# Retention on one core: steps of 64 tokens in bursts of 256, each burst in three parts, in place of chunks of 128 and 64

## The chip, the core and the metric

The kernel runs on one core of a Trainium2 chip. TensorE (PE in the profile) multiplies matrices into PSUM, VectorE (DVE), ScalarE (ACT) and GpSimd (POOL) do the rest, SyncE (SP) issues the DMAs. The metric is the device time of one execution in microseconds.

## What is computed

A retention (linear attention with a decay per head), then two feed-forward parts. Batch 8, 8 heads, 576 tokens, head dimension 64, so 4608 tokens of 512 columns:

```python
scores = scale * np.matmul(q, k.transpose(0, 1, 3, 2))
gamma = 1.0 - 2.0 ** (-5.0 - np.arange(H, dtype=np.float32))
rel = pos[:, None] - pos[None, :]
Dmat = np.where(rel >= 0, gamma[:, None, None] ** rel[None, :, :], 0.0)
attn = np.matmul(scores * Dmat[None, :, :, :], v)          # then tokens x 512
h = np.maximum(np.maximum(x @ w1, x @ w2), x @ w3);  x = h @ w_out
a = x @ w1;  b = x @ w2;  out = ((a * b) @ w3) @ w_out      # second set of weights
```

## The kernel before

The retention is computed chunk by chunk with a running state. `chunk_list` cuts the 4608 tokens into chunks of 128, and of 64 where a batch (576 tokens) or a block of 512 tokens ends. For a chunk, TensorE computes the scores of its own keys and queries (L414), VectorE multiplies them with a triangular mask (`decay`, L421), TensorE multiplies them with v (`own_output`, L429) and adds what earlier chunks contribute through the state (`state_output`, L436); `gather` (L449) multiplies k with v to what the chunk adds to the state, and `update` (L455, L457) adds that to the state and multiplies it with the decay over the chunk. Decays are folded into q (`scale_q`, L394) and v (`scale_v`, L397) beforehand, on POOL. q and k come turned, by VectorE's transpose of 32x32 squares (`turn`, L400). The result lies in PSUM (tile `o`) and is split by `x_hi` (ACT) and `x_lo` (DVE) into two parts for the products that follow. All matmuls of the retention are float32, on quarters or halves of the array: scores and state output use 64 rows by 64 columns, own output and gather 128 rows (the keys) by 64 columns for chunks of 128.

The first feed-forward part (`products`, L537) runs block by block, nine blocks of 512 tokens, 18 products of twelve 128x512 matmuls each; `maximum` (L547) reads them. What runs beside it is ordered by a plan: `when(t, step)` gives a step a due time, counted in products, and the steps are emitted in order of time. Each engine works through its steps in that order. For the first two blocks (the opening, `EARLY`) the order is written out by hand in `ORDER`; a `+` there takes the next step of the plan.

Behind the opening the 31 remaining chunks (25 of 128 tokens, 6 of 64) go in pairs, the bursts. Everything that TensorE has to do for one burst stands together: at `t_o` gather, own output and state output of a pair, and with them (`t = behind`, the `t_o` of the burst before) the scores of the pair after it. So TensorE leaves the products 17 times: 16 times for a burst, with the first scores by themselves. The due times around it are 10.5 products ahead of the scores for the fetch of q and k, 5 for scaling q, 0.6 to 1.6 behind the scores for the decays, 8.5 ahead of the output for v and k, 3.5 for scaling v. Where the two chunks of a pair belong to different batches, q and k are fetched and turned for each by itself.

PSUM: products, scores and gathered sums share six banks in turn; `o` has two banks of its own, for one burst at a time. While products run, the weights of the later parts are converted from float64 on ACT and DVE (L179 to L188, L245). Later parts (L768 on) aren't touched.

Of the kernel before, what the change touches and what calls it, by code (L numbers as in the profile page):

```python
# [9 lines left out]
F32 = mybir.dt.float32  # L10
# [12 lines left out]
P = 128  # L23
# [15 lines left out]
eq8 pr0.7 mx0.6 up7 sl9 jn9 wo11 sc7 kp0.1 mx0.7 + hi9 sl10 sc8 pr0.8 + da7 wo12 db7 da8 db8 ou7 lo9 jn10 mx0.8 hi10  # L39
ga8 pr0.9 ft14 xh7 lo10 ft15 xl7 kp0.2 ft16 up8 ou8 mx0.9 + + + pr0.10 xh8 xl8 + pr1.0 mx0.10 sl11 jn11 wo13 pr1.2  # L40
sl12 ft17 mx1.0 sl13 hi11 wo14 lo11 pr1.6 sl14 wo15 jn12 wo16 jn13 pr1.3 jn14 mx1.6 hi12 hi13 lo12 hi14 pr1.1 lo13
mx1.3 lo14 sl15 jn15 wo17 pr0.11 mx1.1 hi15 mx1.2 lo15 kp1.0 sl16 pr1.5 mx0.11 jn16 kp0.3 sl17 hi16 pr1.4 lo16 jn17
hi17 pr1.9 mx1.4 mx1.5 lo17 kp1.1 pr0.12 mx1.9 pr1.7 mx0.12 + + + + mx1.7 + + + pr1.8 + + + + + pr0.15 mx1.8 + kp1.2
pr0.17 + + + + pr0.16 mx0.15 + mx0.16 + + mx0.17 kp0.5 + + + + + + + pr0.14 + + + pr1.10 + + + + + + + + pr0.13 mx1.10
pr1.12 mx0.13 mx0.14 + kp0.4 + + + + + pr1.11 mx1.12 + + mx1.11 + + + kp1.3 + + + + + + + pr1.15 + + + + + + + + + + +
pr1.16 mx1.15 + + + + pr1.13 + + + + mx1.16 pr1.14 mx1.13 + + + + pr1.17 mx1.14 + kp1.4 + + + + + + + mx1.17 + kp1.5 +
+ + + + + + + + + + + + + + + + +
# [20 lines left out]
JOINT = ((128,), (128, 128), (128, 64), (64, 128))  # L68
JOINT_AT = [sum(sum(x) for x in JOINT[:n]) // 32 for n in range(len(JOINT) + 1)]


def decay_tables():

    gamma = 1.0 - 2.0 ** (-5.0 - np.arange(H))
    i = np.arange(P)
    own = gamma.reshape(2, G)[i // D]
    qs = np.zeros((P, JOINT_AT[-1], G))
    sd = np.zeros((P, 2, G))
    for n, sizes in enumerate(JOINT):
        R = sum(sizes) // 32  # L80
        for T in range(R):
            at = i % 32 * R + T
            at = np.where(at < sizes[0], at, at - sizes[0])
            qs[:, JOINT_AT[n] + T] = own ** at[:, None] / np.sqrt(D)
    for j, c in enumerate((128, 64)):
        sd[:, j] = own ** c
    vd = gamma[None, :] ** -i[:, None].astype(np.float64)
# [7 lines left out]
def tile_retention_maxout_bilinear(ctx: ExitStack, tc, a, out):  # L95
# [170 lines left out]
    n_q = JOINT_AT[-1]  # L266
    tables = cst.tile([P, (n_q + 2) * G + H], F32, name="tables")
    qs = tables[:, :n_q * G].rearrange("p (T h) -> p T h", h=G)
    sd = tables[:, n_q * G:(n_q + 2) * G].rearrange("p (j h) -> p j h", j=2)
    vd = tables[:, (n_q + 2) * G:]  # L270
# [8 lines left out]
    def below(dst, base, rows, op=ALU.is_ge):  # L279
        nc.gpsimd.affine_select(out=dst, in_=dst, compare_op=op, fill=0.0, base=base, pattern=[[1, P]], channel_multiplier=-rows)  # L280
# [12 lines left out]
    def make_mask():  # L293
        nc.gpsimd.memset(mask, 1.0)
        below(mask, 0, 1)

# [32 lines left out]
    def attend(n, t=None, t_o=None, slot=0, pair=None, sizes=None):  # L329
        pair = {} if pair is None else pair  # L330
# [9 lines left out]

        def raw_qk(x):
            return double(x, t, 8, G, 32)[:, 4 * slot:4 * slot + R]

        def turned_qk(x):
            v = double(x + "t", t, 2, G, P, **{"bufs": 1} if x == "k" else {}).rearrange("p s h t -> p (s h t)")
            if sizes and len(sizes) == 2:
                return v[:, :G * 32 * R].rearrange("p (h t) -> p h t", h=G)
            return v[:, G * P * slot:G * P * slot + G * c].rearrange("p (h t) -> p h t", h=G)

        def fetch_qk():  # L350
            for x in "qk":
                for g in range(2):
                    for e in range(2):
                        o = D * g + 32 * e
                        load(raw_qk(x)[o:o + 32], a[x][b, G * g:G * g + G, t0:t0 + 32 * R, 32 * e:32 * e + 32].rearrange(
                            "h (t T) d -> t T h d", T=R))

        def fetch_kv():
            fetch_v()
            if not last:  # L360
                kn = at.tile([P, H, D], F32, tag="kn", name="kn", bufs=4)
                load(kn[:c], a["k"][b, :, t0:t0 + c, :].rearrange("h t d -> t h d"))
                z["kn"] = kn.rearrange("p (g h) d -> p g h d", g=2)
# [28 lines left out]
        def scale_q():  # L392
            q, at_T = raw_qk("q"), JOINT_AT[JOINT.index(sizes)]
            nc.gpsimd.tensor_tensor(q, q, qs[:, at_T:at_T + R].unsqueeze(3).to_broadcast([P, R, G, 32]), ALU.mult)  # L394

        def scale_v():
            nc.gpsimd.tensor_tensor(z["v"], z["v"], vd.unsqueeze(2).to_broadcast([P, H, D]), ALU.mult)  # L397

        def turn(x):
            nc.vector.transpose(out=turned_qk(x).rearrange("p h (t T) -> p T h t", T=R), in_=raw_qk(x))  # L400

        def take():
            at_t = sizes[0] if slot and len(sizes) == 2 else 0
            for x in "qk":
                z[x + "t"] = turned_qk(x)[:, :, at_t:at_t + c]

        def scores():
            if t is not None:
                take()
# [59 lines left out]
        if t is None:  # L469
            steps = dict(fk=(fetch_pairs, "k", "kn"), fq=(fetch_pairs, "q", "q"), fv=(fetch_v,), tk=(swap, "k"), tq=(swap, "q"),  # L470
                         ek=(settle, "k"), eq=(settle, "q"), sc=(scores,), da=(decay, 0), db=(decay, 1), sv=(scale_v,),
                         ou=(output,), xh=(x_hi,), xl=(x_lo,))
            if not last:
                steps.update(ga=(gather,), up=(update,))
            for kind, step in steps.items():
                early(f"{kind}{n}", *step)
            return
        lag = 2.0 * slot
        R = sum(sizes) // 32
        follows = slot == 1 and len(sizes) == 2  # L480
        if not follows:
            when(max(t - 10.5, 4.4) + lag, fetch_qk)
            when(t - 5 + lag, scale_q)
            when(t - 4.8 + lag, turn, "q")
            when(t - (2.8 if len(sizes) == 2 else 4.7) + lag, turn, "k")
        when(t_o - 8.5 + 0.75 * lag, fetch_kv)
        when(t, scores)
        when(t + 0.6 + 0.35 * lag, decay, 0)
        when(t + 0.9 + 0.35 * lag, decay, 1)
        if not last:  # L490
            when(t_o - 0.04, gather)
            when(t_o - 0.035 if slot == 0 else t_o + 0.5, update)
        when(t_o - 3.5 + 0.5 * lag, scale_v)
        when(t_o - 0.03, own_output)
        if not first:
            when(t_o - 0.01 if slot == 0 else t_o + 0.005, state_output)
        when(t_o + 0.5 + 0.25 * lag, x_hi)
        when(t_o + 1 + 0.25 * lag, x_lo)

    by_block = {}  # L500
    for n, (b, t0, *_) in enumerate(chunks):
        by_block.setdefault((b * S + t0) // N1, []).append(n)
    due = []
    for t, ns in by_block.items():
        for i, n in enumerate(ns):
            if t < EARLY:
                attend(n)
            else:

                due.append((n, t, T_BLK * (t - 1) - 0.52 + T_BLK * i / len(ns)))  # L510
    bursts = []
    for m in reversed(range(0, len(due), 2)):
        some = due[m:m + 2]
        t_o = min(some[-1][2], T_BLK * some[0][1] - 2.52, bursts[0][0] - 7 if bursts else NT)
        bursts.insert(0, (int(t_o + 0.52) - 0.52, some))
    behind = bursts[0][0] - 9
    for t_o, some in bursts:
        t_o = min(t_o, behind + 8) if behind > 0 and t_o != bursts[0][0] else t_o
        pair = {}
        own = tuple(chunks[n][2] for n, _, _ in some)  # L520
        joint = len(some) == 2 and chunks[some[0][0]][0] == chunks[some[1][0]][0]
        for slot, (n, _, _) in enumerate(some):
            attend(n, behind, t_o, slot, pair, own if joint else own[slot:slot + 1])
        behind = t_o
# [843 lines left out]
```

## Time and profile before

| | us |
|---|---|
| median of 3 runs | 1216.07 (1215.03 to 1216.69) |
| the profiled execution | 1216.72 |
| its span, first to last instruction | 1215.0 |
| TensorE busy | 1205.9 |
| VectorE busy | 915.8 |
| ScalarE busy | 507.1 |
| GpSimd busy | 304.3 |

The opening lasts until about 76 us, the nine blocks of products until about 530 us; the retention's last work for TensorE stands at 488 us. Busy time counts when an engine had an instruction in work. Matmuls overlap in the array, so the cost of one on TensorE is the distance from its start to the next start, not its duration.

### The profile page before, as it was taken

Reading aid. Unit: us, or ns where it says so; the run is one execution under the profiler, and the core shown is the slowest. Engines: PE = TensorE matmul, PEld = TensorE weight load, DVE = VectorE, ACT = ScalarE, POOL = GpSimd, SP = SyncE. Lnnn points to the kernel's source line nnn. Section 1 sums busy time; section 2 is a strip of 40 time slices with the busy share of each in tenths; the row PEclk is TensorE's granted clock in tenths of the full one; section 3 lists DMA queues with packets and bytes.
Section 4 is the critical chain, followed back from the end, with each engine's and each line's share of the span. In section 5 each row is a group of like instructions: output and inputs, shape, how many; then the busy total and the mean of one; then the engine's idle time right before and its main releaser. Section 6 shows DMA issues by size and latency. Waiting matters only on the chain. (4 is left out here: it accounts for less than half of the span.)

```text
span 1215.0 us, 22807 instructions
## 1 busy us (share of the span) xinstructions
PE 1205.9 (99%) x8900; PEld 1079.6 (89%) x8900; DVE 915.8 (75%) x1236; ACT 507.1 (42%) x873; POOL 304.3 (25%) x246
## 2 busy tenths in 40 slices
PE   8999999999999999999999999999999999999998
PEld 6888888888888888888889888888998888999998
DVE  5896767777768888467998467775766777998996
ACT  3661232323322322234566454443443344555554
POOL 2201212112111110000000315544244442344443
PEclk9999999999999999999999999999999999999999
DMA  9957799988987784534743733324233324455553
GB/s 206 245 143 136 189 227 206 229 191 200 209 221 166 172 206 121 175 113 165 236 172 130 252 129 131 122 105 135 101 113 130 137 66 145 156 166 168 179 166 105
DMA packets 303824, 199.36 MB, mean 164 GB/s; under 512 B 207330, under 2 KB 261346, under 8 KB 303716
## 3 DMA queue, kind: packets, MB, share of 16 engines
q1 hardware_dynamic: 303716, 197.90, 58.6%
q8 instruction: 70, 1.15, 0.4%
q14 instruction: 38, 0.31, 0.1%
HBM read 131.79 MB, written 66.06 MB: 163 GB/s over the span
## 5 line engine op out<-in xcount | busy, mean ns | idle before, releaser
L537 PE MATMUL ps_h<-xh,w1h 128*128 128x512 f32 (+1 forms) x664 | 250.4, 379 | 0.0
L537 PE MATMUL ps_h<-xh,w1l 128*128 128x512 f32 (+1 forms) x664 | 247.7, 375 | 0.5 <-DVE w1l L103 0.3
L537 PE MATMUL ps_h<-xl,w1h 128*128 128x512 f32 (+1 forms) x664 | 167.2, 375 | 0.0
L537 PEld LDWEIGHTS ps_h<-xh,w1h 128*128 128x128 f32 x664 | 125.7, 189 | 19.5 <-issue 2.2
L537 PEld LDWEIGHTS ps_h<-xh,w1l 128*128 128x128 f32 x664 | 126.0, 190 | 17.0 <-DVE w1l L103 1.0
L537 PEld LDWEIGHTS ps_h<-xl,w1h 128*128 128x128 f32 x664 | 124.0, 190 | 16.7
L547 DVE TENSOR_TENSOR hb<-ps_h,hb 128x512 f32<-128x512 f32 (+1 forms) x110 | 74.8, 680 | 74.1 <-PE ps_h L537 56.5
L1222 POOL TENSOR_TENSOR c<-c 128x512 f32<-128x512 f32 (+1 forms) x60 | 82.8, 1380 | 169.4 <-DVE c L1214 131.1
L1209 ACT ACTIVATE snap<-ps_x 128x512 f32<-128x512 f32 (+1 forms) x100 | 55.4, 554 | 158.8 <-PE ps_x L768 148.7
L100 ACT ACTIVATE hb<-ps_h 128x512 f32<-128x512 f32 (+1 forms) x56 | 32.5, 580 | 178.9 <-PE ps_h L537 178.9
L397 POOL TENSOR_TENSOR v<-v,tables 128x512 f32<-128x512 f32 x40 | 44.3, 1110 | 167.9 <-DMA v<-in_v_dram 148.7
L100 ACT ACTIVATE xh<-o 128x512 fp32r<-128x512 f32 (+1 forms) x40 | 22.2, 554 | 131.8 <-PE o L436 94.2
L179 ACT ACTIVATE e<-raw 128x512 f32<-128x512 f32 x64 | 55.4, 866 | 23.6 <-DMA raw<-in_moe_w_out_dram 8.2
L421 DVE TENSOR_TENSOR p<-sc,mask 128x512 f32<-128x512 f32 (+1 forms) x80 | 48.4, 629 | 13.7 <-PE sc L414 13.5
L394 POOL TENSOR_TENSOR q<-q,tables 128x512 f32<-128x512 f32 (+2 forms) x19 | 28.9, 1520 | 107.4 <-DMA q<-in_q_dram 97.3
L180 ACT ACTIVATE r<-raw 128x512 int32<-128x512 uint32 x64 | 54.8, 857 | 0.0
L188 DVE SCALAR_TENSOR_TENSOR m<-raw,m 128x512 int32<-128x512 int32 x64 | 53.3, 836 | 0.5
L185 DVE CUSTOM_DVE_ANT_0 m<-m,r 128x1024 uint16<-128x1024 uint16 x64 | 48.1, 752 | 7.3 <-ACT r L180 0.4
L103 POOL TENSOR_TENSOR ol<-raw,oh 128x512 fp32r<-128x512 f32 x1 | 1.3, 1277 | 205.1 <-ACT oh L100 205.1
L1214 DVE TENSOR_TENSOR c<-ps_x,snap 128x512 f32<-128x512 f32 (+1 forms) x40 | 25.2, 635 | 35.2 <-ACT snap L1209 11.1
L1214 DVE TENSOR_TENSOR c<-ps_v,snap 128x512 f32<-128x512 f32 (+1 forms) x40 | 24.8, 633 | 27.3 <-PE ps_v L768 12.9
L768 PE MATMUL ps_x<-t4h,a 128*128 128x512 f32 (+1 forms) x160 | 44.0, 360 | 0.3 <-DVE a L103 0.3
(305 smaller groups left out, 3269.9 us busy)
## 6 DMA issues: line engine op xcount, KB each, us to landing
raw<-in_moe_w_dram SPq DMA_DIRECT2D x50, 512.0 KB, 5.2
zr<-g_d SPq DMA_DIRECT2D x18, 1024.0 KB, 6.0
g_d<-c SPq DMA_DIRECT2D x64, 256.0 KB, 2.3
zr<-z_d SPq DMA_DIRECT2D x28, 512.0 KB, 6.1
h_d<-hb SPq DMA_DIRECT2D x54, 256.0 KB, 4.1
b<-h_d SPq DMA_DIRECT2D x16, 768.0 KB, 6.1
out_dram<-ob SPq DMA_DIRECT2D x35, 256.0 KB, 2.0
v<-in_v_dram SPq DMA_DIRECT2D x32, 256.0 KB, 5.5
```

The source lines that it names most:

```text
L100: nc.scalar.activation(dst, src, AF.Copy)
L179: nc.scalar.activation(z["e"], raw[:, :, 1].bitcast(F32), AF.Copy, scale=2.0 ** -112)
L180: nc.scalar.activation(z["r"], raw[:, :, 0].bitcast(U32), AF.Copy, scale=2.0 ** -29)
L185: nc.vector.tensor_tensor(z["m"], z["m"], z["r"], ALU.add)
L188: nc.vector.scalar_tensor_tensor(z["m"], z["hi"], -0x80000000, z["m"], ALU.bitwise_and, ALU.bitwise_or)
L397: nc.gpsimd.tensor_tensor(z["v"], z["v"], vd.unsqueeze(2).to_broadcast([P, H, D]), ALU.mult)
L421: nc.vector.tensor_tensor(z[g][:c, :, :c], z["sc"][g][:c, :, :c], mask[:c, :c].unsqueeze(1).to_broadcast([c, G, c]), ALU.mult)
L537: nc.tensor.matmul(ps[:, cols], l, r, start=n == 0, stop=n == len(mms) - 1)
L547: nc.vector.tensor_tensor(hb, unwoven(ps[:, cols]), hb, ALU.max)
L1209: nc.scalar.activation(t, unwoven(ps[:, :size]), AF.Copy)
L1214: nc.vector.tensor_tensor(r, unwoven(ps[:, :size]), t, ALU.add)
L1222: nc.gpsimd.tensor_tensor(x, x, y, ALU.mult)
```

## The change

Behind the opening the retention runs in steps of 64 tokens (`C`), nine to a batch (`SUBS`), and bursts are 256 tokens aligned to half blocks, whatever batch they lie in: 14 bursts of four steps. A burst holds two slots of 128 tokens with two steps each. Scores are computed only within a step (64 by 64); with `e = 1` own output takes one pairing of steps and heads, with `e = 0` the other, both on quarters of the array; the gather takes one step's 64 keys, also on quarters. The state is kept after every step, within a burst without multiplying it: decays count from the burst's start, in the tables for q (256 positions) and v (two slots), and only the burst's last update multiplies with the decay over 256 tokens. Steps that begin a batch have no state output, and those that close one no gather.

Each burst has three parts in TensorE's order, each between products: scores at `t_s` (2 behind the output of the burst before), gather and own output for `e = 1` at `t_g = t_s + 3`, state output and own output for `e = 0` at `t_o`. A copy of one column on ACT (`order`) stands between the two parts that write `o`. The upper half of the mask's first 64 columns is repeated in its lower half (`make_squares`). The places of `+` in `ORDER` change: 100 in place of 113. The opening's own steps (`attend_first`) stay as they were.

```diff
+C = 64
+SUBS = S // C
+R_T = 8
...
+def pieces_of(t0, size):
+    out, at = [], 0
+    while at < size:
+        b, t = divmod(t0 + at, S)
+        n = min(size - at, S - t)
+        out.append((b, t, n, at))
+        at += n
+    return out
...
+    at = i[:, None] % 32 * R_T + np.arange(R_T)
+    qs = own[:, None] ** at[:, :, None] / np.sqrt(D)
+    sd = np.stack([own ** c for c in (128, 64, 256)], 1)
+    vd = np.stack([gamma[None, :] ** -(e * P + i[:, None]).astype(np.float64) for e in range(2)], 1)
...
+    own_first = [(0, 0), (1, 1), (0, 1), (1, 0)]
+    squares = mask[:, :C]
...
+        def fetch_qk():
+            for x in "qk":
+                z[x] = at.tile([P, R_T, G, 32], F32, tag=x, name=x)
+                for g in range(2):
+                    for e in range(2):
+                        for b, t0, size, first in pieces_of(n * PAIR, PAIR):
+                            o = D * g + 32 * e + first // R_T
+                            load(z[x][o:o + size // R_T], a[x][b, G * g:G * g + G, t0:t0 + size, 32 * e:32 * e + 32].rearrange(
+                                "h (t T) d -> t T h d", T=R_T))
...
+        def scores():
+            z["sc"] = [bank("sc").rearrange("p (n h t) -> p n h t", n=2, h=G) for g in range(2)]
+            for slot in range(2):
+                for h in range(G):
+                    for g, s in own_first:
+                        nc.tensor.matmul(z["sc"][g][rows_of(s), slot, h], of("kt", g, h, slot, s), of("qt", g, h, slot, s), start=True, stop=True)
...
+        def gather():
+            z["st"] = [bank("st").rearrange("p (n h d) -> p n h d", n=2, h=G) for s in range(2)]
+            for slot in range(2):
+                for h in range(G):
+                    for g, s in own_first:
+                        if not closes(4 * n + 2 * slot + s):
+                            nc.tensor.matmul(z["st"][s][rows_of(g), slot, h], z["kn", slot][rows_of(s), g, h],
+                                             z["v", slot][rows_of(s), G * g + h], start=True, stop=True)
+
+        def own_output(e):
+            if e == 1:
+                z["o"] = attn_ps.tile([P, 2, 2, G, C], F32, tag="o", name="o")
+            for slot in range(2):
+                for r in range(2):
+                    for s in range(2):
+                        g = s ^ e
+                        for u in range(2):
+                            h = 2 * r + u
+                            nc.tensor.matmul(z["o"][rows_of(u), g, slot, 2 * r + s], z["v", slot][rows_of(s), G * g + h], z[g][rows_of(s), slot, h],
+                                             start=e == 1 and slot == 0 and r == 0, stop=slot == 1 and r == 1, skip_group_check=e == 0)
+            if e == 1:
+                nc.scalar.activation(order, z["o"][:, 0, 1, 3, :1], AF.Copy)
+
+        def state_output():
+            for slot, s, m in subs:
+                if begins(m):
+                    continue
+                for r in range(2):
+                    for g in range(2):
+                        for u in range(2):
+                            h = 2 * r + u
+                            nc.tensor.matmul(z["o"][rows_of(u), g, slot, 2 * r + s], before[m][rows_of(g), h], of("qt", g, h, slot, s),
+                                             start=False, stop=False, skip_group_check=True)
...
+            if not begins(m):
+                nc.vector.tensor_tensor(new, sums, before[m], ALU.add)
+                if ends:
+                    nc.vector.tensor_tensor(new, new, ratio, ALU.mult)
+            elif ends:
+                nc.vector.tensor_tensor(new, sums, ratio, ALU.mult)
+            else:
+                nc.scalar.activation(new, sums, AF.Copy)
...
+        when(max(t_s - 10.5, 4.4), fetch_qk)
+        when(t_s - 5, scale_q)
+        when(t_s - 4.8, turn, "q")
+        when(t_s - 2.8, turn, "k")
+        when(t_s, scores)
+        when(t_s + 0.6, decay, 0)
+        when(t_s + 0.9, decay, 1)
+        when(t_g, gather)
+        when(t_g + 0.01, own_output, 1)
+        for i, sub in enumerate(subs):
+            when(t_g + 0.5 + 0.3 * i, update, *sub)
+        when(t_o, state_output)
+        when(t_o + 0.01, own_output, 0)
+        for slot in range(2):
+            when(t_g - 8 + 1.5 * slot, fetch_kv, slot)
+            when(t_g - 3 + slot, scale_v, slot)
+            when(t_o + 0.5 + 0.5 * slot, x_hi, slot)
+            when(t_o + 1 + 0.5 * slot, x_lo, slot)
...
+    for n in reversed(range(EARLY * N1 // PAIR, NT // PAIR)):
+        t, i = divmod(n * PAIR, N1)
+        t_o = min(T_BLK * (t - 1) + 3.48 + T_BLK * i // N1, bursts[0] - 9 if bursts else NT)
+        bursts.insert(0, t_o)
```

## Rows read from the trace of the kernel before

**Rows 1.** The page: busy us per engine, and TensorE's granted clock in 40 slices

```profile
PE 1205.9 (99%) x8900; PEld 1079.6 (89%) x8900; DVE 915.8 (75%) x1236; ACT 507.1 (42%) x873; POOL 304.3 (25%) x246
...
PEclk9999999999999999999999999999999999999999
```

**Rows 2.** Waits of PE: who waited for whom, us in total, times, longest

```profile
PE sc L414 <- DVE qt L390: 1.4, 2, 1.0
```

**Rows 3.** Windows: length, busy us (instructions) of PE, PEld, DVE, ACT, POOL; clock, DMA, GB/s

```profile
150.00:200.00 50.00, 50.00 (x461) 44.04 (x460) 35.74 (x52) 15.90 (x23) 9.49 (x10) 1.00 0.98 225
...
400.00:440.00 40.00, 40.00 (x347) 35.18 (x345) 35.89 (x45) 11.73 (x17) 5.61 (x6) 1.00 0.78 174
```

**Rows 4.** Chain of work that ended last: start us, us, twelve matmuls of 128x512

```profile
902.41 2.59 PE ps_x L768 x12
```

**Rows 5.** Groups by line and shape on PE, 100 to 490 us: busy us, mean ns

```profile
L537 PE MATMUL ps_h<-xh,w1h 128*128 128x512 f32 x480 | 183.9, 383 | 0.0
L537 PE MATMUL ps_h<-xh,w1l 128*128 128x512 f32 x480 | 182.2, 380 | 0.0
L537 PE MATMUL ps_h<-xl,w1h 128*128 128x512 f32 x481 | 123.6, 380 | 0.0
L414 PE MATMUL sc<-qt,kt 64*64 64x128 f32 x800 | 25.1, 270 | 0.0
```

**Rows 6.** Timeline of PE around the first scores: start us, us until its end

```profile
104.94 1.03 PE L537 MATMUL ps_h<-xl,w1h 128*128 128x512 f32 x4
105.90 1.98 PE L414 MATMUL sc<-qt,kt 64*64 64x128 f32 x64
107.80 0.48 PE L537 MATMUL ps_h<-xh,w1h 128*128 128x512 f32 x1
108.12 0.38 PE L537 MATMUL ps_h<-xh,w1l 128*128 128x512 f32 x1
```

**Rows 7.** Timeline of PE, one full burst

```profile
334.31 1.15 PE L449 MATMUL st<-v,kn 128*64 128x64 f32 x32
335.30 1.92 PE L429 MATMUL o<-p,v 128*64 128x128 f32 x32
337.14 0.67 PE L436 MATMUL o<-qt,s 64*64 64x128 f32 x16
337.63 1.93 PE L414 MATMUL sc<-qt,kt 64*64 64x128 f32 x64
339.38 0.62 PE L436 MATMUL o<-qt,s 64*64 64x128 f32 x16
```

**Rows 8.** Timeline of PE, state output with 64 columns and what follows it

```profile
208.26 0.46 PE L436 MATMUL o<-qt,s 64*64 64x64 f32 x16
208.54 0.40 PE L414 MATMUL sc<-qt,kt 64*64 64x128 f32 x8
```

**Rows 9.** Timeline of PE in the opening, with a stall named in brackets

```profile
29.14 0.67 PE L436 MATMUL o<-qt,s 64*64 64x128 f32 x16 [0.73 <-issue]
```

**Rows 10.** Groups by line and shape on DVE, 100 to 490 us

```profile
L421 DVE TENSOR_TENSOR p<-sc,mask 128x512 f32<-128x512 f32 x50 | 33.4, 685 | 11.3 <-PE sc L414 11.2
...
L400 DVE STREAM_TRANSPOSE kt<-k 128x1024 f32<-128x1024 f32 x6 | 12.4, 2067 | 0.0
...
L457 DVE TENSOR_TENSOR s<-s,tables 128x256 f32<-128x256 f32 x18 | 10.0, 557 | 0.6
...
L400 DVE STREAM_TRANSPOSE kt<-k 128x512 f32<-128x512 f32 x6 | 9.5, 1586 | 0.0
...
L455 DVE TENSOR_TENSOR s<-st,s 128x256 f32<-128x256 f32 x18 | 7.6, 422 | 15.8 <-PE st L449 12.9 <-PE o L436 2.8
L421 DVE TENSOR_TENSOR p<-sc,mask 64x256 f32<-64x256 f32 x12 | 4.7, 405 | 0.0
L457 DVE TENSOR_TENSOR s<-st,tables 128x256 f32<-128x256 f32 x6 | 2.5, 421 | 5.4 <-PE st L449 5.4
```

**Rows 11.** Timeline of DVE behind the scores that end at 339.38

```profile
345.97 0.72 DVE L421 TENSOR_TENSOR p<-sc,mask 128x512 f32<-128x512 f32 x1
```

More of the change, by code (lines that the diff above doesn't have):

```diff
@@ L65, in chunk_list @@
     return out
-JOINT = ((128,), (128, 128), (128, 64), (64, 128))
-JOINT_AT = [sum(sum(x) for x in JOINT[:n]) // 32 for n in range(len(JOINT) + 1)]
+C = 64
[9 more added lines that the diff above has]
+    return out
 def decay_tables():
@@ L260, in tile_retention_maxout_bilinear @@
         add(EARLY * T_BLK - 6.5 + u * ((n_blk - 1 - EARLY) * T_BLK + 2.5) / len(rest))
[L266 to L270, printed above, removed]
+    tables = cst.tile([P, (R_T + 3) * G + 2 * H], F32, name="tables")
+    qs = tables[:, :R_T * G].rearrange("p (T h) -> p T h", h=G)
+    sd = tables[:, R_T * G:(R_T + 3) * G].rearrange("p (j h) -> p j h", j=3)
+    vd = tables[:, (R_T + 3) * G:].rearrange("p (j h) -> p j h", j=2)
+    order = cst.tile([P, 1], F32, name="order")
     mask = cst.tile([P, P], F32, name="mask")
@@ L279, in below @@
     def below(dst, base, rows, op=ALU.is_ge):
-        nc.gpsimd.affine_select(out=dst, in_=dst, compare_op=op, fill=0.0, base=base, pattern=[[1, P]], channel_multiplier=-rows)
+        nc.gpsimd.affine_select(out=dst, in_=dst, compare_op=op, fill=0.0, base=base, pattern=[[1, dst.shape[-1]]], channel_multiplier=-rows)
     def warm():
@@ L295, in make_mask, with make_squares @@
         below(mask, 0, 1)
+    def make_squares():
+        nc.gpsimd.memset(mask[C:, :C], 1.0)
+        below(mask[C:, :C], 0, 1)
     def load_rows():
@@ L327, in double, with attend_first @@
         return doubles[tag, key]
-    def attend(n, t=None, t_o=None, slot=0, pair=None, sizes=None):
-        pair = {} if pair is None else pair
+    def attend_first(n):
+        pair, slot, t = {}, 0, None
         b, t0, c, first, last = chunks[n]
@@ L339, in attend @@
         z = {}
[L341 to L363, printed above, removed]
         def fetch_v():
@@ L390, in settle @@
                 nc.vector.tensor_tensor(z["qt"][:, :, :c], z["qp"][:, :, :c], turned[:, :, :c], ALU.mult)
-        def scale_q():
-            q, at_T = raw_qk("q"), JOINT_AT[JOINT.index(sizes)]
-            nc.gpsimd.tensor_tensor(q, q, qs[:, at_T:at_T + R].unsqueeze(3).to_broadcast([P, R, G, 32]), ALU.mult)
         def scale_v():
[L397 to L405, printed above, removed]
+            nc.gpsimd.tensor_tensor(z["v"], z["v"], vd[:, 0].unsqueeze(2).to_broadcast([P, H, D]), ALU.mult)
         def scores():
-            if t is not None:
-                take()
             z["sc"] = [bank("sc").rearrange("p (h t) -> p h t", h=G) for g in range(2)]
@@ L467, in x_lo @@
             low(nc.vector, parts(xl), z["o"][:, :, :, :c], parts(xh))
[L469 to L489, printed above, removed]
@@ L490, in attend @@
-        if not last:
[L491 to L507, printed above, removed]
-            else:
-                due.append((n, t, T_BLK * (t - 1) - 0.52 + T_BLK * i / len(ns)))
-    bursts = []
[L512 to L524, printed above, removed]
+        steps = dict(fk=(fetch_pairs, "k", "kn"), fq=(fetch_pairs, "q", "q"), fv=(fetch_v,), tk=(swap, "k"), tq=(swap, "q"),
+                     ek=(settle, "k"), eq=(settle, "q"), sc=(scores,), da=(decay, 0), db=(decay, 1), sv=(scale_v,),
+                     ou=(output,), xh=(x_hi,), xl=(x_lo,))
@@ new lines, in attend_first, with rows_of, begins, closes @@
+        if not last:
+            steps.update(ga=(gather,), up=(update,))
+        for kind, step in steps.items():
+            early(f"{kind}{n}", *step)
+    n_first = 0
+    while chunks[n_first][0] * S + chunks[n_first][1] < EARLY * N1:
+        attend_first(n_first)
+        n_first += 1
+    own_first = [(0, 0), (1, 1), (0, 1), (1, 0)]
+    squares = mask[:, :C]
+    def rows_of(x):
+        return slice(D * x, D * x + D)
+    def begins(m):
+        return m % SUBS == 0
+    def closes(m):
+        return m % SUBS == SUBS - 1
@@ L527, in tile_retention_maxout_bilinear @@
+    bursts = []
+    for n in reversed(range(EARLY * N1 // PAIR, NT // PAIR)):
+        t, i = divmod(n * PAIR, N1)
+        t_o = min(T_BLK * (t - 1) + 3.48 + T_BLK * i // N1, bursts[0] - 9 if bursts else NT)
+        bursts.insert(0, t_o)
+    t_s = bursts[0] - 9 + 2
+    when(t_s - 6, make_squares)
+    when(t_s, hand_over)
+    for n, t_o in enumerate(bursts):
+        attend(EARLY * N1 // PAIR + n, t_s, t_s + 3, t_o)
+        t_s = t_o + 2
     hbs = {}
```

83 lines of the change are left out of this document (63 added, 20 removed).

## The prediction

> **What bounds the kernel now.** The page comes first. TensorE is busy for 1205.9 of the 1215.0 us, at the full granted clock in every slice, while VectorE has a quarter of the span free [rows 1]. So I ask whether TensorE is held up by anyone, and the waits of PE say hardly: the longest entry in total is 1.4 us, in the opening [rows 2], and from 76 to 490 us the view lists none. In the windows of the stretch that the change rewrites (100 to 490 us) PE is busy for all of every window, while DVE goes up to 35.89 of 40 us and the DMA engines to 0.98 [rows 3]. TensorE's own stream sets the time there: whatever is taken out of it comes off the end, as long as VectorE and the DMAs still deliver.
>
> A busy PE is not yet a price list, since one matmul's duration (380 ns) holds the filling and draining that its neighbours overlap. I price by start to start. Twelve 128x512 matmuls take 2.59 us, so 0.2157 us each [rows 4]. In 100 to 490 us there are 480 + 480 + 481 = 1441 of them [rows 5], 310.8 us; the other 390 - 310.8 = 79.2 us belong to attention. Summing the 17 visits of attention to TensorE, each from where the next product would have started, gives 79.4 us; I use that.
>
> A float32 matmul is two instructions: 25 chunks of 128 with 16 score matmuls each make x800 [rows 5]. What one costs is read from a visit:
> - Scores alone, 64 instructions of 64x64 with 128 columns: the last four products start at 104.94, so the next would at 105.80; scores start at 105.90, the next product at 107.80, and the one after it 0.32 instead of 0.216 later [rows 6]. That is 2.00 + 0.10 = 2.10 us. In the middle of a visit 64 such instructions take 337.63 to 339.38 = 1.75 us, sixteen rounds of 0.109 us in which the four quarters of the array work side by side [rows 7]. So a visit costs 2.10 - 1.75 = **0.36 us** beside its columns.
> - Own output, 128 rows by 64: only two side by side. 32 instructions take 335.30 to 337.14, 1.84 us, sixteen pairs of 0.109 us and 0.09 for the change of tile shape [rows 7].
> - The gather has 64 columns: 32 instructions in 0.99 us, with 0.05 for the visit's first pair [rows 7], so 0.058 to 0.059 us a pair; I use 0.0584, at which the check below closes.
> - State output with 64 columns, four quarters: 16 instructions from 208.26 to 208.54 [rows 8], 0.28 us of which 0.05 is the first round after a change of shape; 0.058 us a round.
>
> Check on the whole: scores 800/4 x 0.1092 + 96/2 x 0.0584 = 24.6 us; own output (400 and 96 instructions, in pairs) 24.6; state output (320 and 80, in fours) 9.9; gather (336 + 48, in pairs) 11.2. Together 70.4 us. The remaining 9.0 us are 17 visits: 0.36 for the first and 0.51 for most of the others, which change from the 128x64 to the 64x64 shape on the way (0.15). The prices close.
>
> **The change, part by part, on TensorE.** There are 14 bursts of 256 tokens, 56 steps of 64.
> - Scores: 32 matmuls of 64 columns a burst, 64 instructions, 16 rounds; 14 x 16 = 224 rounds. The score blocks above the diagonal go.
> - Own output: both parts together 64 instructions, now 64x64 and so four side by side: 224 rounds.
> - Gather: 64 instructions a burst. The 7 steps that close a batch are left out, but they idle half the array for their slot and save no round: 224.
> - State output: 50 steps (6 begin a batch) of 16 instructions, 200 rounds.
>
> 872 rounds x 0.0584 = 50.9 us against 70.4. The gain is in scores and own output (24.6 to 13.1 each); gather and state output get dearer by 1.9 and 1.8 us.
> - Visits: 14 bursts in three separated parts are 42 instead of 17. Nothing in them has the 128x64 shape, so I take 0.36 each: 15.1 us against 9.0. The bounds are 0.33 (first visit with a quicker tail) and 0.51.
>
> Sum: 50.9 + 15.1 = 66.0 us against 79.4, **13.4 us less**.
>
> What each quarter sustains is the unknown that matters: 64-column rounds of four stand in the trace only 16 instructions long; now 64 to 128 follow each other. The near bound is 0.058 us a round, the far one the rate of the long runs of scores, 1.75/64 = 27.3 ns an instruction [rows 7]. I take the near one, as it is the same shape and count of columns, and because after the one stall for instructions (0.73 us in the opening) the state output ran on at its usual rate [rows 9].
>
> One rule of the Trainium skill speaks against this. The trace shows 16 instructions of 64 columns in 0.28 us, 17.5 ns each [rows 8]. The skill (TensorE: Matmul & The Clock Gate, The HAM clock gate) says that starts never come closer than about 25 ns however small N is, and TensorEngine Tiling (Instruction Overhead) warns not to take the tiling from a dimension that is already small. By 25 ns the 3376 new instructions would take an estimated 84 us instead of 51; across the quarters the row contradicts it.
>
> **The other engines.** VectorE: 62 decays (33.4 + 4.7 us) become 28 of about 0.685, 19.2 us [rows 10]. The updates go from 20.1 us to about 25 (43 adds at 0.42 and some 13 multiplications at 0.42 to 0.557 [rows 10]). Transposes and the low parts stay within a few us. So VectorE gets lighter by some 15 to 20 us, which is hidden: PE doesn't wait for it. Four first steps move to ScalarE, a quarter busy there, with 14 one-column copies that only order writes. POOL loses its memsets and gains one small mask step ahead of the first scaling of q, far from its use. SP issues about as many transfers (214 instead of 213 for q, k and v by my count), of the same short packets; I price them at nothing, hidden by lead times as long as before (5 products from fetch to scaling). If that cover fails, PE waits at the gather.
>
> New waits on PE: the first part of own output comes three products after the scores, and waits for the decay on VectorE. Until then 3 x 2.59 + 0.36 + 0.93 = 9.1 us pass. Now the last decay of a burst ends at 346.69, 7.3 us after its scores [rows 11], and that one is planned later than the new one, which needs no second slot. The cover shrinks from some 15 us to several, but holds. Queued behind that wait on PE would be the next products. State output waits for three updates, four products (10.4 us) after the gather; before the change it waits inside the visit, where only the scores cover it. The opening loses 13 places for later work and gets others; there VectorE loses a transpose (three at about 1.58 become one of 2.06 in one place [rows 10]). I take zero, bounds minus 1 and plus 3 us.
>
> **The sum against the times.** The profiled execution is 1216.72 us, 1.72 beyond its span; less 13.4 that is 1203.3. It lies 0.65 above the median of 1216.07, so the time is 1216.07 - 13.4 = **1202.7 us**. I count 0.2% (2.4 us) as what a measurement of this kernel tells from no change.
>
> **The rivals.**
> 1. The quarters don't hold their rate (slower). After 16 instructions of a part, the rest go at 27.3 ns: 672 x 14.6 + 2704 x 27.3 ns = 83.6 us, with visits 98.7, so 19.3 us more: 1235. It decides where the mean goes over (79.4 - 15.1)/3376 = 19.0 ns. For it: no long run shown, and more instructions per us than anywhere. Against: four rounds at full rate [rows 8]. The skill's 25 ns, named above, gives an estimated 1236 in the same way. Chance 0.06.
> 2. New waits. Three parts a burst with shorter cover, VectorE at 0.9 in 400 to 440 us and the DMAs near full [rows 3]. If each of the 14 bursts loses 0.3 to 0.8 us, plus up to 3 in the opening: 4 to 14 us, so 1207 to 1217. Chance 0.11.
> 3. Visits at the dear price: 42 x 0.15 = 6.3 us more, 1209. Against: the 0.15 belongs to the 128x64 shape, which is gone. Chance 0.08.
> 4. A little more gain: visits at 0.33, an opening with less idle time: 1200 to 1201. Chance 0.03.
>
> **How the numbers follow.** The forecast has 0.72, with a range of its own of 1200.5 to 1206 (rounds up to 0.063, visits 0.33 to 0.38). Faster by over 0.2% holds it, rivals 3 and 4 and most of rival 2: 0.89. Within 0.2%: the end of rival 2, 0.04. Slower: rival 1 and a little of 2, 0.07. The range is 1199.5 to 1210, which leaves out rival 1 and the upper part of rival 2.
>
> **What the changed profile would show.** Right: PE still without waits behind the opening; 42 visits; 64 scores of 64 columns in about 0.93 us and a visit with them alone in 1.3; gather and own output 1.9 us; the rest of the kernel alike but earlier by 13 us. Wrong: rounds of 64 columns well over 0.06 us (rival 1); PE idle at the own or state output with DVE named, or at the gather with POOL or a DMA (rival 2); visits whose start and tail exceed 0.36 us (rival 3).

## The result, and the profile after

The changed kernel takes **1202.85 us** (median of 6 runs, 1200.65 to 1204.52) against 1216.38 for the kernel before beside it (6 runs, 1214.47 to 1218.76): a ratio of 0.989, 95% interval 0.987 to 0.991. The forecast was 1202.7. The profiled execution took 1202.30 us, 1.7 of it beyond its span of 1200.6.

The page of the changed kernel, to be laid beside [rows 1]:

```profile
PE 1191.8 (99%) x10100; PEld 1059.9 (88%) x10100; DVE 894.8 (75%) x1202; ACT 506.3 (42%) x888; POOL 298.1 (25%) x228
...
PEclk9999999999999999999999999999999999999999
```

TensorE is still the engine that is never free: 14.1 us less busy, with 1200 matmuls and as many weight loads more. Who is waited for, beside [rows 2]:

```profile
PE sc L386 <- DVE qt L376: 1.7, 3, 1.0
...
PE sc L521 <- DVE kt L511: 1.1, 1, 1.1
```

The second row is the only wait in attention behind the opening. The groups of attention on TensorE, 95 to 482 us (busy us, mean ns, idle before), beside [rows 5]:

```profile
L546 PE MATMUL o<-p,v 64*64 64x64 f32 x896 | 18.9, 219 | 0.0
L521 PE MATMUL sc<-qt,kt 64*64 64x64 f32 x896 | 16.3, 221 | 1.1 <-DVE kt L511 1.1
L534 PE MATMUL st<-v,kn 64*64 64x64 f32 x784 | 16.2, 222 | 0.0
L559 PE MATMUL o<-qt,s 64*64 64x64 f32 x800 | 14.9, 221 | 0.0
```

The counts are those of the prediction, all in one shape. (784 is the gather without the closing steps.) One burst, in the timeline of PE (start us, us until its end), beside [rows 7]:

```profile
123.63 0.81 PE L639 MATMUL ps_h<-xl,w1h 128*128 128x512 f32 x3
124.37 1.16 PE L521 MATMUL sc<-qt,kt 64*64 64x64 f32 x64
125.47 0.48 PE L639 MATMUL ps_h<-xh,w1h 128*128 128x512 f32 x1
125.79 0.38 PE L639 MATMUL ps_h<-xh,w1l 128*128 128x512 f32 x1
...
129.89 1.03 PE L639 MATMUL ps_h<-xl,w1h 128*128 128x512 f32 x4
130.84 1.16 PE L534 MATMUL st<-v,kn 64*64 64x64 f32 x64
131.82 0.65 PE L546 MATMUL o<-p,v 64*64 64x64 f32 x32
132.40 0.48 PE L639 MATMUL ps_h<-xh,w1h 128*128 128x512 f32 x1
...
137.78 1.16 PE L559 MATMUL o<-qt,s 64*64 64x64 f32 x64
138.76 0.65 PE L546 MATMUL o<-p,v 64*64 64x64 f32 x32
```

Read start to start, as in the prediction. The three matmuls of a product at 123.63 would let a fourth start at 124.28; scores start 0.09 later, the next matmul of a product at 125.47, and the one after it 0.32 instead of 0.216 later: 1.29 us for the visit. By the prices of the prediction it is sixteen rounds of 0.0584 (0.93) and a visit of 0.36. Gather with own output takes 1.75 us in the same way, state output with own output 1.76.

Over the whole trace, from the span's start to the start of TensorE's last matmul, 1211.69 us became 1197.33, **14.36 less**. Attention behind the opening went from 79.42 us in 17 visits to 66.95 in 42, which is 12.47. The opening gave about 1.6 us, all the rest 0.3.

### The profile page after: what moved, and what is told of

The parts are those of the page before. It is cut to its first block, busy times and chain, and to the rows that moved or that the text cites. A ratio compares the mean times of both kernels' runs of the same rounds, so it can differ in the third digit from the quotient of the medians.

```text
span 1200.6 us, 25154 instructions
## 1 busy us (share of the span) xinstructions
PE 1191.8 (99%) x10100; PEld 1059.9 (88%) x10100; DVE 894.8 (75%) x1202; ACT 506.3 (42%) x888; POOL 298.1 (25%) x228
## 3 DMA queue, kind: packets, MB, share of 16 engines
q8 instruction: 79, 1.29, 0.5%
## 4 chain that ended last, share of the span: by engine, by line
PE 95%; DVE 2%; DMA 1%; ACT 1%; issue 0%; SPq 0%; DVEq 0%; POOL 0%; ACTq 0%; POOLq 0%
PE ps_h L639 35%; PE ps_x L870 23%; PE ps_y L870 11%; PE ps_v L870 6%; PE ps_X L870 5%; PE ps_w L870 3%; PE ps_Y L870 3%; PE ps_V L870 1%; PE sc L521 1%; PE st L534 1%; PE o L546 1%; PE o L559 1%; PE o L401 1%; PE sc L386 1%; DMA raw<-in_moe_w_out_dram 1%
## 5 line engine op out<-in xcount | busy, mean ns | idle before, releaser
L507 POOL TENSOR_TENSOR v<-v,tables 128x512 f32<-128x512 f32 x28 | 31.0, 1108 | 223.5 <-DMA v<-in_v_dram 204.0
L186 ACT ACTIVATE r<-raw 128x512 int32<-128x512 uint32 x64 | 52.2, 815 | 0.0
L503 POOL TENSOR_TENSOR q<-q,tables 128x1024 f32<-128x1024 f32 x14 | 27.6, 1970 | 96.7 <-DMA q<-in_q_dram 68.9
L870 PE MATMUL ps_v<-b21h,a 128*128 128x512 f32 (+1 forms) x160 | 43.8, 359 | 0.1
```

Of the source, the lines that this page charges most:

```text
L186: nc.scalar.activation(z["r"], raw[:, :, 0].bitcast(U32), AF.Copy, scale=2.0 ** -29)
L507: nc.gpsimd.tensor_tensor(v, v, vd[:, slot].unsqueeze(2).to_broadcast([P, H, D]), ALU.mult)
L870: nc.tensor.matmul(ps, l, r, start=start and j == 0, stop=stop and j == len(mms) - 1, skip_group_check=again)
```

## The experiments

The theory was that of the prediction: the time follows TensorE's stream, 0.0584 us for a round of four quarters and 0.36 us for each visit. The rivals were that the quarters lose their rate in long runs (rival 1), and that new waits or VectorE set the time (rival 2). All line numbers are those of the changed kernel, moved by a line or three where an edit adds some. The kernel before, beside which each was timed, took 1215.29 us (19 runs) for the repeat, the doubled scores, and two visits and one visit a burst; 1215.76 (7 runs, on another chip) for the doubled decays, four visits, and the two kernels that change from the third burst on; 1217.36 (one run) for the last two. Between these groups the ratios are to be compared, not the times.

**The changed kernel once more**, for an equal to compare with.

> The changed kernel as it is, timed beside the three others on the same chip: 1202.9 by every theory. It is the base for the differences of e1, e2 and e3.

1201.21 us (1200.7 to 1202.42), ratio 0.988 (0.986 to 0.989). Attention takes 65.79 us in 42 visits and there is no wait in it behind the opening: the one of 1.1 us above belongs to a single execution. In that one the timeline of DVE reads

```profile
139.75 0.43 DVE L190 TENSOR_SCALAR m<-e 128x512 int32<-128x512 int32 x1 [2.98 <-ACT e L185]
140.51 0.69 DVE L191 CUSTOM_DVE_ANT_0 m<-m,r 128x1024 uint16<-128x1024 uint16 x1 [0.33 <-ACT r L186]
141.12 2.06 DVE L511 STREAM_TRANSPOSE kt<-k 128x1024 f32<-128x1024 f32 x1
```

that of ACT

```profile
139.04 0.68 ACT L185 ACTIVATE e<-raw 128x512 f32<-128x512 f32 x1 [6.27 <-DMA raw<-in_moe_w_out_dram]
```

and that of PE

```profile
143.33 1.16 PE L521 MATMUL sc<-qt,kt 64*64 64x64 f32 x64 [1.13 <-DVE kt L511]
```

The transposition of k stood behind a conversion step on VectorE that waited 2.98 us for ScalarE, and ScalarE waited for a transfer. This is rival 2's mechanism, once, for 1.1 us.

**Each score product twice.** If the quarters fall back in runs longer than 16, 128 instructions in a row cost far more than twice 64.

```
-                    for g, s in own_first:
+                    for g, s in own_first + own_first:
```

> The changed kernel with every score matmul behind the opening issued twice (the second writes the same values): 896 instructions of 64 columns more, in runs of 128 instructions. If TensorE's stream sets the time and the quarters hold their rate in long runs: 224 rounds x 0.0584 = 13.1 us more than the changed kernel, about 1216, which is the time before. If long runs fall to 27.3 ns an instruction: 24.5 us more or above. If TensorE has hidden slack: clearly less than 13 us.

1215.47 us (10 runs, 1213.88 to 1217.54), ratio 1.000 (0.999 to 1.001): 14.3 us above the changed kernel. Attention takes 78.81 us, 13.02 more, as expected; the opening, which the edit doesn't touch, ended 2.0 us later in this trace than in that of the repeat (first scores behind it at 108.57 and 106.61). The timeline of PE:

```profile
127.01 2.09 PE L521 MATMUL sc<-qt,kt 64*64 64x64 f32 x128
129.04 0.48 PE L639 MATMUL ps_h<-xh,w1h 128*128 128x512 f32 x1
129.36 0.38 PE L639 MATMUL ps_h<-xh,w1l 128*128 128x512 f32 x1
```

128 instructions start within 129.04 - 127.01 = 2.03 us, where 64 took 125.47 - 124.37 = 1.10: 0.93 us for 64 more, 14.5 ns each. By rival 1's 27.3 ns they would have taken 1.75. Rival 1 falls.

**VectorE charged with 19 us.** Every decay is computed twice, which takes VectorE back to more than it did before the change.

```
-            nc.vector.tensor_tensor(z[g]..., squares..., ALU.mult)
+            for _ in range(2):
+                nc.vector.tensor_tensor(z[g]..., squares..., ALU.mult)
```

> The changed kernel with each of its 28 decays behind the opening issued twice on VectorE (same values), 28 x 0.68 = 19 us more there, about what the change takes off VectorE. If TensorE's stream alone sets the time: as the changed kernel, 1201.2 in the last comparison, within 1.5 us. If the lighter VectorE carried a part of the gain: 3 us more or above, with waits of TensorE that name VectorE.

1202.77 us (1200.79 to 1202.99), ratio 0.989 (0.987 to 0.991): by the ratio no different from the changed kernel (0.988 in the repeat); by the time 1.56 above it, just over the 1.5 expected. Attention takes 65.75 us, again without a wait behind the opening; here too the opening ended 2.0 us later (108.64). VectorE is busy for 916.7 us, 0.9 more than before the change. What VectorE saves by the change is hidden, as forecast, and so is that much more.

**Four visits a burst.** The first part of own output goes one product further back, away from the gather.

```
-        when(t_g + 0.01, own_output, 1)
+        when(t_g + 1.01, own_output, 1)
```

> The changed kernel with the first part of own output a product behind the gather, so that a burst has four visits: 56 instead of 42, the same columns. Price of 0.36 us a visit: 14 x 0.36 = 5.0 us more than the changed kernel, 1206.2. If visits are free: 1201.2. Shorter runs of instructions can't stall more on the supply of instructions, so nothing else is expected to change.

1206.6 us (1205.33 to 1207.27), ratio 0.993 (0.991 to 0.994). Twelve visits more are found, not the 14 expected (in two bursts the two parts stood together all the same), and attention takes 70.01 us: (70.01 - 65.79)/12 = **0.352 us a visit**, with the same instructions. A visit costs what the prediction said, measured by itself.

**Two visits a burst.** If 0.35 us are paid for each visit, fewer should pay. Scores of the next burst directly behind the state and own output:

```
+    t_g = t_s + 3
...
-        attend(EARLY * N1 // PAIR + n, t_s, t_s + 3, t_o)
-        t_s = t_o + 2
+        attend(EARLY * N1 // PAIR + n, t_s, t_g, t_o)
+        t_s, t_g = t_o + 0.02, t_o + 5
```

> The changed kernel with the scores of the next burst placed directly behind the second part of own output, so that they share a visit; everything else of a burst is timed as in the changed kernel. TensorE leaves the products 29 times instead of 42. If the stream of TensorE sets the time and a visit costs 0.36 us beside its columns: 13 x 0.36 = 4.7 us less than the changed kernel, about 1198. If the gain of the change came from the lighter VectorE, with TensorE only seeming busy, fewer visits bring nothing: 1203. If the changed kernel has hidden waits at the visits, more than 4.7 us comes back or a new wait takes it.

1199.91 us (1198.32 to 1200.54), ratio 0.986 (0.985 to 0.988). Attention takes 63.59 us in 29 visits. That holds a stall of 1.8 us inside one visit, which the waits name "issue", and the opening ended about 2 us later than in the repeat of the changed kernel (first scores behind it at 108.83 and 106.61); kernels whose opening has the same order vary as much. So of 4.6 us for 13 visits saved, attention shows 2.2 and the median 1.3.

**One visit a burst**, all parts one behind the other, the updates moved with them. In one line of `ORDER` some places of `+` move too.

```
-        when(t_g + 0.01, own_output, 1)
+        when(t_o, own_output, 1)
...
-            when(t_g + 0.5 + 0.3 * i, update, *sub)
-        when(t_o, state_output)
-        when(t_o + 0.01, own_output, 0)
+            when(t_g + 1.1 + 0.3 * i, update, *sub)
+        when(t_o + 0.006, state_output)
+        when(t_o + 0.008, own_output, 0)
...
-        t_s = t_o + 2
+        t_s, t_g = t_o + 0.002, t_o + 0.004
```

> The changed kernel with all parts in one visit per burst: first part of own output, scores and gather of the next burst, state output, second part of own output. 16 visits instead of 42, the same columns. Visit price 0.36 us: 26 x 0.36 = 9.4 us less than the changed kernel, about 1193.5. New risk: the state output now waits inside the visit for the one-column copy on ScalarE, with only scores and gather (1.87 us) to cover it; if ScalarE is behind by another conversion each time, up to 0.5 us of each of 14 visits comes back (1200). If visits are free: 1203.

**1227.5 us** (10 runs, 1216.13 to 1230.32), ratio 1.009 (1.006 to 1.011): slower than the kernel before, and 34 us off what I expected. This theory of visits alone falls. The profiled execution, 1222.75 us, is one of the quicker ones. Attention takes 85.54 us in it. The waits of PE:

```profile
PE o L559 <- issue: 14.0, 6, 4.1
PE o L546 <- issue: 7.5, 4, 3.1
PE st L534 <- POOL v L507: 1.8, 1, 1.8
...
PE st L534 <- issue: 1.0, 1, 1.0
...
PE o L559 <- ACT order L549: 0.3, 1, 0.3
```

22.5 of the 24.3 us in the first four of these rows wait for nothing that the profile shows. The copy on ScalarE, the risk named beforehand, is waited for once, for 0.3 us. One of the stalls in the timeline:

```profile
226.66 1.11 PE L534 MATMUL st<-v,kn 64*64 64x64 f32 x64
227.59 1.09 PE L559 MATMUL o<-qt,s 64*64 64x64 f32 x59
232.79 0.28 PE L559 MATMUL o<-qt,s 64*64 64x64 f32 x3 [4.11 <-issue]
```

The stall comes in the middle of one loop, after 59 of its 64 matmuls. I numbered TensorE's records in the trace (weight loads, matmuls, semaphore records) from 0. The eleven stalls of this kernel come before records 2753, 3521, 4033, 4801, 5569, 6337, 7617, 8385, 9665, 10433 and 11201: **each is 193 modulo 256**. (Not every wait named "issue" is: one of 0.2 to 0.3 us in the opening of some kernels, the repeat among them, stands elsewhere.) The one of the kernel with two visits is at 4801 as well. Even the stall of 0.73 us in the opening of the kernel before [rows 9] is at record 705, which is 193 modulo 256. The page's queue of instructions, of before and then of after:

```profile
q8 instruction: 70, 1.15, 0.4%
```

```profile
q8 instruction: 79, 1.29, 0.5%
```

A packet has 1.29 MB/79, about 16.3 KB (single ones 16,384 bytes), which over 256 instructions is 64 bytes each. So a new theory: TensorE's instructions arrive in blocks of 256, and work that runs through a block too quickly stops at its end until the next is there. At 14.6 ns for a matmul with its weight load, a block lasts 1.87 us; among products (0.216 us a matmul) 27.6 us. The Trainium skill (Runtime: NRT & Kernel Launch, Instruction fetch mechanics) gives the same block, 16 KiB for 256 instructions, and calls crossing its border mostly hidden; the trace agrees on the block, but here the crossing is not always hidden. In the changed kernel no two borders behind the opening are nearer than 7.05 us, and none shows a stall.

**Two kinds of two or three visits, from the third burst behind the opening on**, now with this theory's costs. First, own output and scores of the next burst in one visit, one product, then gather, state and own output (the decays half a product later):

```
-        when(t_g + 0.01, own_output, 1)
+        when(t_g + 0.01 if i_burst < 3 else t_o, own_output, 1)
...
-        when(t_o, state_output)
-        when(t_o + 0.01, own_output, 0)
+        t_o += 0 if i_burst < 2 else 1
+        when(t_o + 0.002, state_output)
+        when(t_o + 0.004, own_output, 0)
...
+        t_s, t_g = (t_o + 2, t_o + 5) if n < 2 else (t_o + 0.002, t_o + 1)
```

> From the burst of 512 tokens behind the opening's end on, the order of e2 cut in two by one product: own output (first part) and the next scores, a product, then gather, state output and own output (second part); earlier bursts as in the changed kernel, the decays half a product later so that the second part has read the buffer. 32 visits. The stalls of e2 stood at every 256th instruction record of TensorE and nowhere else; if they are the supply of instructions, a product between gives it 2.6 us more and nearly all vanish: 10 x 0.36 = 3.6 us less than the changed kernel, 1197.6, up to 1200 if two or three stalls of 1 us stay, each at such a record. If e2 was slow because the state output waits in the visit for the copy on ScalarE, or for any other engine, these visits keep that (own output and scores still stand within a product of it) and the time stays above 1203.

1200.16 us (1198.83 to 1200.69), ratio 0.987 (0.986 to 0.989). Attention takes 63.64 us in 32 visits, with a stall of 0.7 and one of 0.3 us, each at a block's border. Second, the two visits from above, from the same burst on:

```
...
-        t_s = t_o + 2
+        t_s, t_g = t_o + (2 if n < 2 else 0.02), t_o + 5
```

> As e1, but only behind the opening: the scores of the next burst share the visit of state output from the third burst on, so the order of the opening is that of the changed kernel. 31 visits. Visit price: 11 x 0.36 = 4.0 us less than the changed kernel, 1197.2, and none of the 2 us that e1 lost in the opening; up to 2 us more for a visit of 306 instructions in which two of the 256-instruction marks fall.

1200.8 us (1199.1 to 1202.3), ratio 0.988 (0.986 to 0.989). Attention takes 64.52 us, with one stall of 2.3 us at record 4801, in the timeline of PE:

```profile
191.52 1.09 PE L521 MATMUL sc<-qt,kt 64*64 64x64 f32 x58
194.96 0.34 PE L521 MATMUL sc<-qt,kt 64*64 64x64 f32 x6 [2.34 <-issue]
```

Of the 4.6, 3.5 and 3.9 us that the visits saved by price, attention shows 2.2, 2.2 and 1.3; stalls took most of the rest. None of these three kernels differs clearly from the changed one in its time.

**The borders moved.** That the stalls stand at borders is so far a coincidence of numbers. On top of the edit above, 22 of the 32 score products of one burst at 106 us are issued again, 88 records more, and nothing else changes. All later borders then fall elsewhere in the same work.

```
-            for slot in range(2):
-                for h in range(G):
-                    for g, s in own_first:
-                        nc.tensor.matmul(...)
+            todo = [(slot, h, g, s) for slot in range(2) for h in range(G) for g, s in own_first]
+            for slot, h, g, s in todo + (todo + todo)[:22 if n == EARLY * N1 // PAIR else 0]:
+                nc.tensor.matmul(...)
```

> The kernel of e7_two_late with 22 of the 32 score products of the burst at 106 us issued again: 44 matmuls and 44 weight loads more, about 0.65 us (44 x 14.6 ns), and nothing else changed; every later record of TensorE stands 88 places further back. Theory of the instruction blocks (TensorE's instructions come in blocks of 256 records, and a second block border within some 2 to 4 us stops TensorE): the stall of 2.56 us at 192.4 is gone, for no two borders stand in that visit any more; the only places with two borders under 4.3 us apart are the visits of state output, own output and scores at about 221, 331 and 442 us (1.86 us apart each), and at least one of the three has a stall of over 0.3 us, at a record that is 193 modulo 256; no other stall behind 110 us. Rival, that the stall belongs to the work that stands at 190 us (a transfer or ScalarE): the stall of over 1 us stays in the visit at about 190 us and none comes at the three places.

The timeline of PE with 88 records more, at the old place and at a new one:

```profile
194.20 0.65 PE L545 MATMUL o<-p,v 64*64 64x64 f32 x32
194.66 1.11 PE L520 MATMUL sc<-qt,kt 64*64 64x64 f32 x64
195.71 0.48 PE L639 MATMUL ps_h<-xh,w1h 128*128 128x512 f32 x1
...
443.73 0.92 PE L520 MATMUL sc<-qt,kt 64*64 64x64 f32 x49
445.25 0.46 PE L520 MATMUL sc<-qt,kt 64*64 64x64 f32 x15 [0.60 <-issue]
```

All 64 scores run through where 2.3 us were lost before, and a stall of 0.6 us stands in one of the three places named beforehand. At the second (223.3) the border has a gap of 0.19 us, and the third (333.7) has none. With 38 products, 152 records:

> The kernel of e7_two_late with 38 score products of the burst at 106 us issued again: 76 matmuls and 76 weight loads more, about 1.1 us, nothing else changed; every later record stands 152 places further back. Theory of the instruction blocks: no stall at 192; two borders under 4.3 us apart only at about 249 (1.91 us), 278 (2.92 us) and 360 us (1.86 us), and at least one of them stalls by over 0.3 us, at a record that is 193 modulo 256; none at 221, 331 or 442 us. Rival of the place: the stall stays in the visit at about 190 us.

The timeline of PE with 152 records more:

```profile
277.20 1.11 PE L520 MATMUL sc<-qt,kt 64*64 64x64 f32 x64
...
279.22 0.38 PE L639 MATMUL ps_h<-xh,w1h 128*128 128x512 f32 x1
280.57 0.48 PE L639 MATMUL ps_h<-xh,w1l 128*128 128x512 f32 x1 [0.98 <-issue]
```

Again nothing at 192, and one stall, at the second of the three places named, record 7105 (27 x 256 + 193), this time in the products behind the visit. Of the other two none. The times, one run each, were 1202.19 and 1199.78 us. Both kernels did what the theory of blocks said and what the rival excluded: **the stall goes with the border, not with the work**.

The distance of two borders doesn't say which one stalls: 1.9 us after the one before it, 249 and 360 went through, and the second of the two kernels above (two visits, from the third burst on) lost 0.4 us at a border 6.6 us behind the last one. The traces show what does. Queue q8 has one packet for each border of TensorE: 70 packets where TensorE has 17,944 records, 79 at 20,327 and 80 at 20,423. The first packet starts near the first border (record 193), so I take it for the block behind the second, and so on. Times in us:

| kernel | border at record | border before passed | packet ends | first record behind the border starts | stall |
|---|---|---|---|---|---|
| before [rows 9] | 705 | 21.68 | 27.83 | 29.14 | 0.73 |
| one visit | 5569 | 226.55 | 231.44 | 232.79 | 4.11 |
| two visits, from the third burst on | 4801 | 190.48 | 193.34 | 194.96 | 2.34 |
| the same | 8385 | 333.48 | 338.67 | 340.07 | 0.4 |
| 88 records more | 8385 | 331.84 | 330.74 | 333.70 | none |
| 88 records more | 11201 | 442.53 | 443.92 | 445.25 | 0.60 |
| 152 records more | 6337 | 248.25 | 246.92 | 250.16 | none |
| 152 records more | 7105 | 276.29 | 279.23 | 280.57 | 0.98 |
| 152 records more | 9153 | 360.18 | 359.22 | 362.04 | none |

Of the 936 borders in the twelve traces none is passed sooner than 1.24 us behind the end of its packet, and the stalls of 0.3 us and more at borders end 1.24 to 1.61 us behind it. So a border stalls when its packet is late. What makes one late isn't shown: packets start from 4.5 us ahead of the border before to 6.4 us behind it. Nor did I try to make the supply itself faster or slower.

## Why the prediction was right, step by step

- **Rounds of four quarters** (0.0584 us, from 16 instructions of state output [rows 8]): right. The doubled scores give 13.02/(14 x 16) = 0.0581. The near bound was the right one to take, since the row had the same shape.
- **Visits** (42 at 0.36): right. In the repeat, where nothing waits, (65.79 - 50.9)/42 = 0.355, and 0.352 by the kernel with four visits. The dear price of 0.51 (rival 3) is seen in no visit now that the 128x64 shape is gone: gather and own output together take 1.75 us, 24 rounds and 0.35. The 1.9 us that the prediction named for that visit in the profile was a slip against its own prices, which give 1.40 + 0.36.
- **Closing steps save no gather round**: right. The visit with 48 gather instructions took 1.74 us, with 64 also 1.75.
- **The sum of attention**, 79.4 to 66.0: 65.75 or 65.79 where nothing stalled, 66.95 in the profiled execution, where rival 2 came in once with 1.1 us.
- **The opening at zero, bounds minus 1 and plus 3**: this execution gained about 1.6 us, a little outside. Kernels whose opening has the same order reached the first scores behind it between 106.1 and 108.8 us, so a part of that is chance. The 1.6 and rival 2's 1.1 make up for most of each other by luck: by the profile 14.4 us were gained where 13.4 were forecast, by the medians 13.5.
- **The other engines**: VectorE 21.0 us less busy, forecast 15 to 20. The rows of DVE, 95 to 482 us, beside [rows 10]:

```profile
L511 DVE STREAM_TRANSPOSE kt<-k 128x1024 f32<-128x1024 f32 x14 | 28.8, 2054 | 0.0
...
L525 DVE TENSOR_TENSOR p<-sc,mask 128x512 f32<-128x512 f32 x28 | 18.4, 687 | 7.2 <-PE sc L521 7.2
L576 DVE TENSOR_TENSOR s<-st,s 128x256 f32<-128x256 f32 x43 | 18.1, 421 | 8.4 <-PE st L534 6.4 <-ACT s L582 1.5
L578 DVE TENSOR_TENSOR s<-s,tables 128x256 f32<-128x256 f32 x10 | 6.6, 658 | 0.3
```

28 decays take 18.4 us (forecast 19.2), the updates 25.5 (forecast 25; with two multiplications of 0.8 us together that aren't among these rows). None of it shows in the time, and neither do 19 us more of it.
- **Cover of the new waits**: held. Own output and state output show no idle time before them in the groups above (0.0), so three and four products do cover decay and update.
- **Rival 1** was given 0.06 for a concern that was real in another form. "More instructions per us than anywhere" does not slow the quarters, but it can outrun the supply. The prediction read [rows 9] as a stall after which the rate was as usual; it didn't ask what had stalled there. In this change the three separate parts, of at most 192 records (96 matmuls and their weight loads) with products between them, keep the borders apart. Nothing in the prediction foresaw that; it was luck as far as the supply goes. The margin is thin: in the repeat of the changed kernel the packet for record 4801 ended at 197.08, and the record started 1.30 us later, about as close as where TensorE stalled. What the visits cost (42 x 0.35 = 14.7 us) is thus not simply there for the taking, as the kernel with one visit a burst shows.

## What to carry to other kernels

Price a TensorE-bound stage by starts, not durations: columns by the round that the quarters sustain, and a fixed price for each break in the stream of products; both can be read from the kernel before even if it holds the new shape only 16 instructions long. Small matmuls in long unbroken runs save such breaks and risk the instruction supply: where a wait is named "issue" in the middle of a loop, count the engine's instructions from the start, and if the stalls share a remainder, see when the packets of its instruction queue end, and spread the small matmuls between long ones.

## What the runs showed of the hardware that was not expected

- TensorE can stop at each 256th of its instructions (193 modulo 256 in these kernels), for 0.3 to 4.1 us by the waits, until 1.24 to 1.61 us behind the end of the block's packet. The changed kernel, with borders at least 7.05 us apart behind the opening, never stopped there in its two traces; but in the opening of the kernel before it did with 7.5 us [rows 9], so no interval here is a safe one.
- A stall can cost twice. Windows of the kernel with one visit a burst, before and behind its stall at 232 (length, busy us of PE, PEld, DVE, ACT, POOL, granted clock, DMA share, GB/s):

```profile
215.00:225.00 10.00, 10.00 (x48) 8.66 (x46) 7.67 (x11) 3.70 (x5) 0.93 (x1) 1.00 0.94 199
...
233.53:236.70 3.17, 3.17 (x11) 2.51 (x9) 0.34 (x1) 0.60 (x1) 0.00 (x0) 0.50 0.61 137
236.80:245.00 8.20, 8.20 (x39) 7.18 (x38) 5.89 (x10) 4.16 (x7) 2.09 (x2) 0.99 0.92 259
```

and of the one with two visits from the third burst on:

```profile
195.85:198.60 2.75, 2.75 (x8) 2.19 (x7) 0.76 (x2) 0.00 (x0) 1.83 (x1) 0.50 0.95 149
```

Behind the stalls of 4.1 and 2.3 us the granted clock was 0.50 for some 3 us, the level of 1.2 GHz, and matmuls of products started 0.43 us apart instead of 0.216; so about 1.5 us more are lost. Behind the stalls of 0.6 and 0.98 us in the last two kernels they went on at 0.216 us. The length of the stall alone doesn't decide it: behind those of 3.05 and 2.63 us in the kernel with one visit the granted clock stayed at 1.00. It bears on that kernel's spread: its ten runs go from 1216.13 us, at a mean granted clock of 1.000, to 1230.32 at 0.992; 0.008 below full is by this an estimated 20 us at half the clock, and some 10 us lost.
- Matmuls on quarters of the array can start 14.5 ns apart on average over 128 in a row, with a weight load for each.
